# Sparse attention followed by a routed expert layer: key maxima by halving, wide summary scores, new planner figures and smaller filler multiplications

## The chip, the cores and the metric

The kernel runs on one core of one Trainium2 chip. The metric is the device time of one execution in microseconds (us), as the median of several. A core has a matrix engine (TensorE, written PE in the profile; PEld is its weight load), a vector engine (VectorE, DVE), a scalar engine (ScalarE, ACT), a general engine (GpSimd, POOL), a sync engine (SP), and 16 DMA engines. Each engine works through its own queue in order. A later engine waits for an earlier one by semaphores.

## The reference, cut to what matters

There are two stages. The first is attention with 4 batches, 8 heads, 768 positions and 64 dimensions per head. A query sees keys less than 16 positions away, and 24 block summaries, one for each block of 32 positions: the elementwise maximum of the block's keys and the mean of its values.

```
k_sum = k.reshape(B, H, nb, block, D).max(axis=3)
v_sum = v.reshape(B, H, nb, block, D).mean(axis=3)
scores_l = scale * np.matmul(q, k.transpose(0, 1, 3, 2))      # kept where |i - j| < 16
scores_s = scale * np.einsum('bhsd,bhnd->bhsn', q, k_sum) + np.log(block)
...                                                            # softmax over both, times v and v_sum
```

The second stage takes the attention output as 3072 rows of 512. It makes a soft assignment P to 8 experts, with 8 rounds of row and column normalisation, and adds up over the experts.

```
for e in range(E):
    h = np.maximum(x @ w1[e], 0.0)      # 512 -> 1024
    ye = h @ w2[e]                      # 1024 -> 512
    out += P[:, e:e + 1] * ye
```

## The kernel before, in words

**Tiling.** Two heads make a pair, so there are 16 pairs, 4 for each batch. Keys and queries of a pair are transposed to `kT` and `qT`: 128 partitions (two heads of 64 dimensions) by 768 positions. Scores are made with keys on the partitions. The near scores of 128 keys go against 160 queries (`sg`, L344); the summary scores have the 24 block maxima of each head on the partitions (`ss`, L446, L449, L455). Exponentials run on ACT, masks and normalisation on DVE, and the result is transposed into `xT`, which the experts multiply.

**The summary path.** For a pair `key_max` (L332) reduces `kT`, 24 blocks of 32, to `ks` with one DVE reduction. `key_max_split` (L338) spreads `ks` over two heads into `ksT[:, 0:64]`, zero where a row belongs to the other head. For the 12 pairs after the first batch `summaries_2` (L455) makes two multiplications with that 64-column weight: query half 0 goes to partitions 0 to 63 of one PSUM bank, query half 1 to partitions 64 to 127. For the first batch, half 0 uses `ks` directly (L446) and half 1 uses all 128 columns of `ksT` (L449), of which columns 64 to 127 are zero.

**The first batch.** Pairs 0 to 3 are worked in two halves of the queries, so that the first expert's work can begin early. Keys and values of pair 0 come in float32 through SP and are cast on chip. All else comes through POOL's DMA queue, with a cast, in this order: q of pair 0 (half), k and q of pair 1, of pair 2, v of pair 1, k and q of pair 3, v of pairs 2 and 3, two quarters of expert 0's first weight, the other query halves of the four pairs, the other two quarters, k and q of pair 4, expert 0's second weight `w2`. POOL builds the identity and the band mask between the first of these.

**The planner.** Every piece of work is a unit with an engine, a guessed cost in us, dependencies and a priority (`add`). `Plan.order` simulates the engines with these guesses and at each step issues the unit that can start first; among units that can start within 0.02 us the lowest priority number goes first. What it puts out is the program order of every engine. Nothing is decided at run time: a wrong guess only makes an order that fits the real times less well. For the first batch, `plan.follow` fixes the order on PE, DVE and ACT by lists written out by hand; these lists are not in the change. Loads are units on a virtual DMA engine: a load starts after the one before it and takes its guessed transfer time (`load`, L853 and below).

PSUM banks are rings: tag `m` has three banks (transposes of the first batch, its first summary scores, the fillers, and later expert 0's products), `a` three, `s` one pair.

**Fillers.** `keep_busy(n)` issues n multiplications of a zero tile, 128 x 128 weights by 512 columns, into an `m` bank; nothing reads them. Nine are issued at the start, before any input is there. While the planner runs, each time PE would stand idle for over 0.22 us by its figures, it inserts one more (L1268), as long as an `m` bank is free, until expert 0's first evacuation is placed.

**The rest.** Expert 0 takes plain multiplications (L208, L213), which fill PE while the attention pairs 4 to 15 are made. Experts 1 to 7 use a seven-product scheme (L749, L800). The planner orders all of it.

Of the kernel before, what the change touches and what calls it, by code (L numbers as in the profile page):

```python
# [128 lines left out]
def kernel(  # L129
# [10 lines left out]
    nc = tc.nc  # L140
# [82 lines left out]
    with tc.manual_schedule():  # L223
# [15 lines left out]
        ksT = [attn.tile([128, 128], BF16, name=f"ksT{i}") for i in range(NB)]  # L239
# [90 lines left out]
        def key_max(i):  # L330
            r = i % NB
            nc.vector.tensor_reduce(out=ks[r][:, 0, 0:24],  # L332
                                    in_=kT[r][:].rearrange("p (n w) -> p n w", w=32),
                                    axis=AX.X, op=ALU.max)

        def key_max_split(i):
            r = i % NB
            nc.vector.tensor_tensor(out=ksT[r][:, 0:64].rearrange("p (j n) -> p j n", j=2),  # L338
                                    in0=ks[r][:].to_broadcast([128, 2, 32]),
                                    in1=own[:].to_broadcast([128, 2, 32]), op=ALU.mult)  # L340
# [98 lines left out]
        def summaries(i, h, tag):  # L439
            r = i % NB  # L440
            ss, rhs = bank(tag, "ss"), qT[r][:, W + h * HS:W + (h + 1) * HS]
            at["ss", i, h] = ss
            if i < PB and not h:
                for j in range(2):
                    p = slice(64 * j, 64 * j + 64)
                    nc.tensor.matmul(ss[32 * j:32 * j + 32, 0:HS], lhsT=ks[r][p, 0, :], rhs=rhs[p],  # L446
                                     start=True, stop=True)
                return
            nc.tensor.matmul(ss[:, 0:HS], lhsT=ksT[r][:], rhs=rhs, start=True, stop=True)  # L449

        def summaries_2(i):
            r, ss = i % NB, bank("a", "ss")
            for h in range(2):
                at["ss", i, h] = ss[64 * h:64 * h + 64]
                nc.tensor.matmul(ss[64 * h:64 * h + 64, 0:HS], lhsT=ksT[r][:, 0:64],  # L455
                                 rhs=qT[r][:, W + h * HS:W + (h + 1) * HS], start=True, stop=True)
# [147 lines left out]
        def keep_busy(n):  # L604

            t = bank("m", "idle")
            for _ in range(n):
                nc.tensor.matmul(t[:], lhsT=zeros[:, 0:128], rhs=zeros[:], start=True, stop=True)
# [9 lines left out]
        keep_busy(9)  # L618
# [19 lines left out]
        def constants():  # L638
# [10 lines left out]
            for t in ksT:  # L649
                nc.vector.memset(t[:, 64:128], 0.0)  # L650
# [201 lines left out]
        def load_pair(i, parts="kqv"):  # L852
            old = i - NQ  # L853
            for c in parts:
                if c == "v":
                    load(("v", i), lambda: load_v(i), 1.05, 1.85,
                         [U.get(("A", old, 1)), U.get(("near", old))])
                elif i < PB and c in "qr":
                    h = "qr".index(c)
                    load(("q", i, h), lambda h=h: load_qk(i, 1, h), 0.65, 0.65)  # L860
                else:
                    z = "kq".index(c)
                    load((c, i), lambda z=z: load_qk(i, z), 0.75 if i < PB else 1.65,
                         1.2 if i < PB else 1.55, [U.get(("tr", old, z)), U.get(("tr", old, 2))])

        def pair_start(i, prio):
# [9 lines left out]
            for z in range(0 if i >= BY_DMA else 1 if i < PB else 2):  # L876
                buf = Buffer("m" if i < PB else "a")
                U["tr", i, z] = add("PE", 0.5 if i < PB else 0.34, lambda z=z: tr(i, z),
                                    [U["kq"[z], i], U["ident"]] + (war_k, war_q)[z]
                                    + [U["tr", i, 0] if z else ahead], prio, opens=[buf])  # L880
                U["kT", i, z] = add({"ACT": 0.8, "DVE": 0.95 if i < PB else 0.56}, 0,
                                    lambda z=z: tr_out(U["kT", i, z].on, i, z), [U["tr", i, z]], prio,
                                    uses=[buf])
            U["ks", i] = add("DVE", 0.95, lambda: key_max(i), [U["kT", i, 0], U.get(("km", o))], prio)
# [3 lines left out]
            U["vs", i] = add("PE", 0.4, lambda: block_sums(i),  # L888
# [40 lines left out]
        def pair_whole(i, prio):  # L929
# [23 lines left out]
            U["ss", i, 0] = U["ss", i, 1] = add("PE", 0.22, lambda: summaries_2(i),  # L953
# [68 lines left out]
        U["vf32"] = add("LAND", 0, None, [add("RING", 0, None, [])], lag=5.6)  # L1022
# [3 lines left out]
        load_pair(1, "kq")  # L1026
        U["band"] = last[0] = add("POOL", 0.7, band_constants, [last[0]])
        load_pair(2, "kq")
        load_pair(1, "v")
        load_pair(3, "kq")  # L1030
        load_pair(2, "v")
        load_pair(3, "v")
        for n in range(4):
            load(("w1", n), lambda n=n: load_w1(0, n, 4), 0.85, 1.25)
            if n == 1:
                for i in range(PB):
                    load_pair(i, "r")
        load_pair(PB, "kq")
        load("w2", lambda: load_w2(0), 0.85, 5.0)
# [228 lines left out]
        plan.idle = (0.22, lambda: keep_busy(1), U["rl", 0, 0])  # L1268
# [33 lines left out]
```

The softmax here doesn't subtract the row's maximum and nothing guards it: scores larger than these inputs give would overflow.

## Time and profile before

| what | value |
|---|---|
| median of 5 executions | 668.23 us |
| the five | 667.25, 667.77, 668.23, 668.3, 672.26 us |
| the profiled execution | 672.0 us, span from first to last instruction 670.3 us |
| PE busy | 662.2 us, 99% of the span |
| DVE, ACT, POOL busy | 82%, 62%, 30% |
| chain of work that ended last | PE 98% |
| reductions of `key_max` | 16, 948 ns each |
| summary scores of pairs 4 to 15 | 24 multiplications, 350 ns each |
| fillers | 16 |

The page gives busy time by engine, then the span in 40 slices with the granted PE clock in tenths, then the chain that ended last and the costliest groups. In a timeline row the columns are start, length, engine, line, operation, tiles, shape and count, and in brackets the idle time before it and what ended that. In a table of stretches, each engine has its busy time and count, then come the granted PE clock, the DMA share and GB/s. A matmul's length contains its passage through the array, so rows overlap: the cost of one among others is the distance from start to start.

### The profile page before, as it was taken

What the parts mean: (1) busy time and instruction counts of PE and PEld (TensorE: products, weight loads), DVE (VectorE), ACT (ScalarE), POOL (GpSimd) and SP (SyncE); (2) the same over time, 40 slices, a digit from 0 to 9 for tenths busy, and PEclk for the clock granted to TensorE, in tenths of its full rate; (3) what the DMA queues carried; (4) which work ended last, traced back from release to release, by engine and by line L of the source; (5) the groups of instructions that cost most, each with busy time, mean ns of one, the idle gap of its engine ahead of it and who ended that gap; (6) DMA issues with size and microseconds to landing.
All of it is one profiled execution on the core that took longest, in us unless ns stands there. A gap on an engine that the chain in (4) does not pass through costs nothing.

```text
span 670.3 us, 13244 instructions
## 1 busy us (share of the span) xinstructions
PE 662.2 (99%) x5131; PEld 437.7 (65%) x5131; DVE 547.7 (82%) x1030; ACT 415.0 (62%) x773; POOL 198.3 (30%) x256
## 2 busy tenths in 40 slices
PE   8999999999999999999999999999999999999996
PEld 4666665555676666666666666666666666666665
DVE  6789877798989787788779887888778877988776
ACT  5577876565886666656565556656655656556652
POOL 8899522100031221222132222222222113222123
PEclk7899999999999999999999999999999999999999
DMA  9999961610754738375654756473837465334656
GB/s 167 173 141 146 125 92 30 118 21 1 127 94 80 127 61 128 64 116 90 95 95 65 125 86 104 78 126 53 134 68 121 81 100 95 64 63 111 156 135 198
DMA packets 112542, 67.89 MB, mean 101 GB/s; under 512 B 77920, under 2 KB 90464, under 8 KB 112480
## 3 DMA queue, kind: packets, MB, share of 16 engines
q0 software_dynamic: 94800, 57.46, 64.4%
q1 hardware_dynamic: 17152, 9.58, 5.8%
q8 instruction: 40, 0.66, 0.4%
q14 instruction: 22, 0.18, 0.1%
q10 hardware_dynamic: 528, 0.02, 0.0%
HBM read 52.45 MB, written 6.29 MB: 88 GB/s over the span
## 4 chain that ended last, share of the span: by engine, by line
PE 98%; DMA 1%; DVE 0%; issue 0%; ACT 0%; SPq 0%; DVEq 0%
PE yps L800 22%; PE pA L749 22%; PE pY L800 16%; PE pQ L749 11%; PE hps L208 6%; PE yps L213 6%; PE pR L749 5%; PE sg L344 2%; PE vs L352 1%; PE av L504 1%; PE tkq L300 1%; DMA kvf<-in_v_dram 1%; PE tx L542 1%; PE av L430 1%; PE av L436 1%; PE ss L455 1%
## 5 line engine op out<-in xcount | busy, mean ns | idle before, releaser
L800 PEld LDWEIGHTS <-h 128*128 128x128 f16 x2352 | 230.1, 98 | 89.1 <-issue 1.0
L828 POOL DMA_DIRECT2D out_acc<-y x120 | 101.4, 886 | 372.9 <-ACT y L824 96.2
L824 ACT ACTIVATE y<-pY,P_sb 128x256 f32<-128x256 f32 x168 | 80.0, 477 | 124.2 <-PE pY L800 122.4
L815 DVE SCALAR_TENSOR_TENSOR out_acc<-yps,P_sb,out_acc 128x512 f32<-128x512 f32 x128 | 95.4, 746 | 29.3 <-PE yps L800 29.3
L783 DVE TENSOR_TENSOR h<-h 128x1024 f16<-128x1024 f16 x168 | 109.2, 685 | 1.4
L800 PE MATMUL pY<-w,h 128*128 128x256 f16 x672 | 100.0, 273 | 0.6 <-ACT y L824 0.6
L800 PE MATMUL yps<-w2sum,h 128*128 128x256 f16 x672 | 98.4, 273 | 0.0
L749 PE MATMUL pA<-xT,w 128*128 128x512 f16 x336 | 98.3, 379 | 0.0
L800 PE MATMUL yps<-w,h 128*128 128x256 f16 x672 | 93.2, 273 | 0.0
L815 DVE SCALAR_TENSOR_TENSOR out_acc<-pY,P_sb,out_acc 128x512 f32<-128x512 f32 x84 | 62.9, 749 | 31.5 <-PE pY L800 30.0
L749 PEld LDWEIGHTS <-w 128*128 128x128 f16 x672 | 65.8, 98 | 31.5 <-issue 0.2
L749 PEld LDWEIGHTS <-w1sum 128*128 128x128 f16 x504 | 49.3, 98 | 44.3
L771 DVE CUSTOM_DVE_ANT_0 h<-pQ,snap 128x512 f16<-128x512 f32 x84 | 57.7, 687 | 6.1 <-ACT snap L204 3.6
L771 DVE CUSTOM_DVE_ANT_0 h<-pA,snap 128x512 f16<-128x512 f32 x84 | 57.6, 685 | 5.5 <-PE pA L749 5.2
L199 ACT ACTIVATE h<-pA 128x512 f16<-128x512 f32 x84 | 50.7, 603 | 13.1 <-PE pA L749 12.9
L199 ACT ACTIVATE h<-pR 128x512 f16<-128x512 f32 x84 | 50.1, 596 | 8.6 <-PE pR L749 8.1
L204 ACT COPY pR<-pA 128x512 f32<-128x512 f32 x83 | 47.4, 571 | 7.1 <-PE pA L749 6.0
L800 PE MATMUL pY<-w2sum,h 128*128 128x256 f16 x336 | 50.4, 273 | 0.0
L749 PE MATMUL pQ<-xT,w1sum 128*128 128x512 f16 x168 | 50.0, 379 | 0.0
L749 PE MATMUL pA<-xsum,w 128*128 128x512 f16 x168 | 50.0, 379 | 0.0
L749 PE MATMUL pA<-xsum,w1sum 128*128 128x512 f16 x168 | 50.0, 379 | 0.0
L749 PE MATMUL pQ<-xsum,w1sum 128*128 128x512 f16 x168 | 50.0, 379 | 0.0
(147 smaller groups left out, 859.3 us busy)
## 6 DMA issues: line engine op xcount, KB each, us to landing
out_acc<-y POOLq DMA_DIRECT2D x120, 256.0 KB, 3.4
w<-in_moe_w_dram POOLq DMA_DIRECT2D x15, 1024.0 KB, 10.0
out_dram<-out_acc SPq DMA_DIRECT2D x24, 256.0 KB, 2.5
qst<-in_q_dram POOLq DMA_DIRECT2D x32, 96.0 KB, 5.4
vx<-in_v_dram POOLq DMA_DIRECT2D x15, 192.0 KB, 6.1
kst<-in_k_dram POOLq DMA_DIRECT2D x24, 96.0 KB, 5.5
w<-in_moe_w_dram POOLq DMA_DIRECT2D x4, 256.0 KB, 7.2
kst<-in_k_dram POOLq DMA_DIRECT2D x3, 192.0 KB, 4.6
```

The source lines that it names most:

```text
L199: nc.scalar.activation(out=out, in_=in_, func=AF.Relu, bias=0.0, scale=1.0)
L204: (nc.scalar.copy if eng == "ACT" else nc.vector.tensor_copy)(out=out, in_=in_)
L208: nc.tensor.matmul(hp[:, 0:n], lhsT=w1s[e][:, dk, f * 128:(f + 1) * 128], rhs=xT[:, dk, t0:t0 + n], start=(dk == 0), stop=(dk == KD - 1))
L213: nc.tensor.matmul(yp[:, d], lhsT=h[:, f, c * 128:(c + 1) * 128], rhs=w2s[e][:, f, d], start=(f == 0), stop=(f == KF - 1))
L344: nc.tensor.matmul(dst, lhsT=kT[r][p0:p0 + 64, g * 128:(g + 1) * 128], rhs=qT[r][p0:p0 + 64, g * 128 + l0:g * 128 + l1], start=True, stop= ...
L749: nc.tensor.matmul(dst[:], lhsT=lhsT, rhs=rhs, start=first and k == 0, stop=k == HK - 1, skip_group_check=True)
L771: nc.vector._custom_dve(dve_ops.TENSOR_ADD_SAT, out=ring(e, p, q)[:, q % 2, blk, :], in0=at[src, e, p, q][:], in1=at.pop(("snap", n, e, p, ...
L783: nc.vector.tensor_tensor(out=h[:, :, out_, :], in0=h[:, :, a, :], in1=h[:, :, b, :], op=op)
L800: nc.tensor.matmul(dst[:, d], lhsT=lhsT, rhs=rhs, start=f == 0 and n in (1, 5, 2), stop=f == HF - 1, skip_group_check=True)
L815: nc.vector.scalar_tensor_tensor(out=o, in0=y, scalar=scalar, in1=o, op0=ALU.mult, op1=ALU.add)
L824: nc.scalar.activation(out=at[key][:, d], in_=src, func=AF.Copy, bias=0.0, scale=P_sb[:, t, e:e + 1])
L828: nc.gpsimd.dma_start(out=o, in_=at.pop(("y", e, p, c, key))[:], accum_op=ALU.add)
```

## The change

- `key_max`: in place of one reduction over 32, two elementwise maxima on DVE (32 to 16, 16 to 8 columns for each block, into new tiles `k_max`), then a reduction over 8.
- `ksT` is 192 columns wide, with the maxima in columns 64 to 127 and zeros on both sides. `summaries_2` uses a 128-column weight both times, once columns 64 to 191 and once 0 to 127, and adds the two products in the same bank. L449 reads columns 64 to 191. The zeroing at the start covers all 192 columns.
- Fillers have 128 columns in place of 512: 38 at the start in place of 9, and the planner inserts one for each 0.11 us of planned idle time in place of 0.22.
- The planner gets other figures for the loads' transfer times, for `key_max`, for `summaries_2` and for two units of pair 0. The loads of the first batch are issued from one list; item by item it is the order of before.

```
-            nc.vector.tensor_reduce(out=ks[r][:, 0, 0:24],
-                                    in_=kT[r][:].rearrange("p (n w) -> p n w", w=32),
-                                    axis=AX.X, op=ALU.max)
+            src, w = kT[r][:].rearrange("p (n w) -> p n w", w=32), 16
+            for t in k_max:
+                nc.vector.tensor_tensor(out=t[:], in0=src[:, :, 0:w], in1=src[:, :, w:2 * w], op=ALU.max)
+                src, w = t, w // 2
+            nc.vector.tensor_reduce(out=ks[r][:, 0, 0:24], in_=src[:], axis=AX.X, op=ALU.max)
...
             for h in range(2):
                 at["ss", i, h] = ss[64 * h:64 * h + 64]
-                nc.tensor.matmul(ss[64 * h:64 * h + 64, 0:HS], lhsT=ksT[r][:, 0:64],
-                                 rhs=qT[r][:, W + h * HS:W + (h + 1) * HS], start=True, stop=True)
+                nc.tensor.matmul(ss[:, 0:HS], lhsT=ksT[r][:, 64 - 64 * h:192 - 64 * h],
+                                 rhs=qT[r][:, W + h * HS:W + (h + 1) * HS], start=h == 0, stop=h == 1)
...
-                nc.tensor.matmul(t[:], lhsT=zeros[:, 0:128], rhs=zeros[:], start=True, stop=True)
+                nc.tensor.matmul(t[:, 0:128], lhsT=zeros[:, 0:128], rhs=zeros[:, 0:128], start=True, stop=True)
...
-        keep_busy(9)
+        keep_busy(38)
...
-                nc.vector.memset(t[:, 64:128], 0.0)
+                nc.vector.memset(t[:], 0.0)
...
                 if c == "v":
-                    load(("v", i), lambda: load_v(i), 1.05, 1.85,
+                    load(("v", i), lambda: load_v(i), 1.05, {1: 1.85, 4: 2.9}.get(i, 1.5),
...
-                    load(("q", i, h), lambda h=h: load_qk(i, 1, h), 0.65, 0.65)
+                    load(("q", i, h), lambda h=h: load_qk(i, 1, h), 0.65, 2.65 if i + h == 0 else 0.42)
...
-                         1.2 if i < PB else 1.55, [U.get(("tr", old, z)), U.get(("tr", old, 2))])
+                         0.95 if i < PB else 1.75 if i == PB else 1.38, [U.get(("tr", old, z)), U.get(("tr", old, 2))])
...
-                U["tr", i, z] = add("PE", 0.5 if i < PB else 0.34, lambda z=z: tr(i, z),
+                U["tr", i, z] = add("PE", 0.65 if i == 0 else 0.5 if i < PB else 0.34, lambda z=z: tr(i, z),
...
-            U["ks", i] = add("DVE", 0.95, lambda: key_max(i), [U["kT", i, 0], U.get(("km", o))], prio)
+            U["ks", i] = add("DVE", 0.7, lambda: key_max(i), [U["kT", i, 0], U.get(("km", o))], prio)
...
-            U["vs", i] = add("PE", 0.4, lambda: block_sums(i),
+            U["vs", i] = add("PE", 0.65 if i == 0 else 0.4, lambda: block_sums(i),
...
-            U["ss", i, 0] = U["ss", i, 1] = add("PE", 0.22, lambda: summaries_2(i),
+            U["ss", i, 0] = U["ss", i, 1] = add("PE", 0.33, lambda: summaries_2(i),
...
-        U["vf32"] = add("LAND", 0, None, [add("RING", 0, None, [])], lag=5.6)
+        U["vf32"] = add("LAND", 0, None, [add("RING", 0, None, [])], lag=6.4)
...
-            load(("w1", n), lambda n=n: load_w1(0, n, 4), 0.85, 1.25)
...
+        for c in "k1 q1 b0 k2 q2 v1 k3 q3 v2 v3 w0 w1 r0 r1 r2 r3 w2 w3".split():
...
+                load(("w1", i), lambda i=i: load_w1(0, i, 4), 0.85, 1.3)
...
-        load("w2", lambda: load_w2(0), 0.85, 5.0)
+        load("w2", lambda: load_w2(0), 0.85, 4.4)
...
-        plan.idle = (0.22, lambda: keep_busy(1), U["rl", 0, 0])
+        plan.idle = (0.11, lambda: keep_busy(1), U["rl", 0, 0])
```

## The prediction

> **What bounds the kernel now.** I read the page first, then one-microsecond stretches of the start, then the timelines of PE and DVE around what the change touches.
>
> ```profile
> PE 662.2 (99%) x5131; PEld 437.7 (65%) x5131; DVE 547.7 (82%) x1030; ACT 415.0 (62%) x773; POOL 198.3 (30%) x256
> ...
> PEclk7899999999999999999999999999999999999999
> ...
> PE 98%; DMA 1%; DVE 0%; issue 0%; ACT 0%; SPq 0%; DVEq 0%
> ```
>
> PE is never idle after the first 26 us, and from there the order of the work is worth little: only PE's own work counts. What can be won lies in the first slices, where the clock digit is below 9. The stretches (PE, PEld, DVE, ACT, POOL, then PE clock, DMA share, GB/s) and the PE timeline show that:
>
> ```profile
> 6.00:7.00 1.00, 0.31 (x13) 0.27 (x13) 0.16 (x1) 0.63 (x1) 1.00 (x2) 1.00 1.34 211
> 7.00:8.00 1.00, 0.77 (x12) 0.48 (x8) 1.00 (x2) 0.48 (x1) 1.00 (x3) 0.98 1.28 190
> 8.00:9.00 1.00, 1.00 (x12) 0.40 (x8) 0.62 (x2) 0.00 (x0) 1.00 (x2) 0.50 1.27 165
> ...
> 20.00:21.00 1.00, 1.00 (x14) 0.87 (x15) 0.80 (x1) 0.46 (x1) 0.88 (x2) 0.50 1.44 193
> 21.00:22.00 1.00, 1.00 (x9) 0.62 (x6) 0.39 (x2) 0.54 (x1) 1.00 (x2) 0.70 1.52 193
> 22.00:23.00 1.00, 1.00 (x15) 0.59 (x14) 0.80 (x3) 0.33 (x1) 1.00 (x2) 1.00 2.22 160
> ```
>
> ```profile
> 6.69 0.38 PE L309 MATMUL tkq<-ident,qst 64*64 64x64 bf16 x12 [0.90 <-DMA qst<-in_q_dram]
> 7.00 0.39 PE L608 MATMUL idle<-zeros 128*128 128x512 bf16 x1
> 7.62 0.54 PE L352 MATMUL vs<-vx,m_blk 128*128 128x128 bf16 x6 [0.23 <-DVE vx L204]
> 7.96 0.62 PE L608 MATMUL idle<-zeros 128*128 128x512 bf16 x1
> ```
>
> PE waits 0.90 us for the first queries; at 7.96 us the clock falls to half and returns at 21.6 us, 13.65 us later. In that time PE is busy throughout: at half clock it is the bound, and in the chain of waits the fillers at 7.96, 16.4, 19.3 and 21.4 take 0.43 + 0.54 + 0.43 + 0.73 = 2.1 us of it.
>
> **Which execution the sum is made for.** The profiled execution took 672.0 us (span 670.3 and 1.7 around it), 3.8 above the median 668.23. One of the five, 672.26, stands beside it. At full clock the first batch could end far earlier: the last values land at 16.84 (DMA records), and behind them come their block sums 0.54, DVE 0.28, weighted values 0.9, normalisation 0.75, transpose 0.33, copy 0.36, together 3.2, so 20.0 in place of 26.7, where the last copy into `xT` ends. The 3.8 lies within these 6.7. I read the median execution as one in which the clock stayed up for most of this stretch, but no profile of such a one is shown. I make the sum for both.
>
> **Key maxima.** These are DVE rows, two of the timeline and three groups (busy, mean ns, idle before):
>
> ```profile
> 44.00 0.95 DVE L332 TENSOR_REDUCE ks<-kT 128x24 bf16<-128x768 bf16 x1 [0.20 <-ACT kT L204]
> 44.99 0.22 DVE L338 TENSOR_TENSOR ksT<-ks,own 128x64 bf16<-128x64 bf16 x1
> ```
>
> ```profile
> L488 DVE TENSOR_TENSOR Eh<-erh,band 128x960 bf16<-128x960 bf16 x8 | 5.2, 649 | 0.0
> ...
> L419 DVE TENSOR_TENSOR Ee<-er,band 32x80 bf16<-32x80 bf16 x24 | 4.7, 196 | 0.5
> ...
> L571 DVE TENSOR_REDUCE rs_sb<-P_sb 128x24 f32<-128x192 f32 x8 | 2.8, 353 | 1.8 <-ACT P_sb L566 1.6
> ```
>
> Two bf16 elementwise rows, 960 columns in 649 ns and 80 (in runs of 16) in 196, give 0.515 ns a column on a base of 155. The first maximum (384 columns) then takes 353 ns, the second (192) 254. The last reduction has its own row: 192 columns, 353 ns. Each reads what the one before wrote, and the first two rows show what that costs: L338 starts 0.04 us after L332 ends (34 ns in the records), where an independent operation starts 84 ns before the end. So 353 + 34 + 254 + 34 + 353 = 1028 ns against 953: 0.075 longer. The planner's 0.70 is what comes out if all three overlapped like independent ones. Pairs 4 to 15 lie beside a full PE: cost 0, and with that cover gone 12 x 0.075 = 0.9. For pairs 0 to 3 it is hidden while PE is at half clock; at full clock DVE is the denser queue and it costs 4 x 0.075 = 0.3. The other end is the planner's figure, a gain of 4 x 0.25 = 1.0.
>
> [...]
>
> **Wide summary scores.** These are PE rows around one pair of narrow products:
>
> ```profile
> 93.36 0.34 PE L436 MATMUL av<-Ve,Ee 128*128 128x130 bf16 x3
> 93.63 0.35 PE L455 MATMUL ss<-qT,ksT 128*64 128x384 bf16 x2
> 93.92 0.66 PE L208 MATMUL hps<-xT,w 128*128 128x384 f16 x3
> ```
>
> The two narrow products run side by side (starts 3 ns apart). But from the start of the last full-size product before them to their start it is 150 ns, where 130 columns at full clock need 56, and the next starts 286 ns later. Together 436. Two full-width products cost 163 each (eight L208 of 384 columns take 1.30 in the chain), so 56 + 326 = 382: a gain of 54 ns. Where the neighbour before is the 64-row product L344 (4 of 12 pairs), its own 159 stays and it is 159 + 286 against 159 + 326: a loss of 40. 8 x 54 - 4 x 40 = 0.27 us gained, all on the path, since PE is full there. The ends: 12 x 54 = 0.65 gained, 12 x 40 = 0.5 lost, by the order that comes out.
>
> **Fillers.** The start block: nine of 512 columns took 3.72 us (1.26 to 4.98). 38 of 128 columns at 0.107 us each (three L542 take 0.32 at half clock) need 4.06 if the clock stays low, and end at 5.3, about when the first keys are cast (5.21). With the clock up at 4.54, as here, the last seven take 0.055 each (six L300 take 0.33), and they end at 4.95. Cost 0, at most 0.1. The inserted ones: for 0.22 us of planned idle there was one filler of 0.213 at full clock, 0.43 at half; now there are two of 0.055, or two of 0.107. At half clock they lie on the path: 2.1 us become about 1.5, since gaps of 0.11 to 0.22 now get one too. Gain 0.6 in the profiled execution, 0 at full clock, where they stand in true gaps. The wider zeroing adds four times some 0.04 us to DVE at 2.1 us, ahead of a 0.91 wait: 0.
>
> **Planned load times.** The issue order and the DMAs are the same; what moves is where the planner puts PE work that waits for them. By its figures the chain of transfers starts at 4.45 before and 5.5 after. To the last values it is then 11.1 before, 8.96 after, and with 0.9 to land 16.45 before, 15.36 after; the trace has 16.84. The last quarter of the first weight: 24.05 before, 22.24 after; the trace has 23.69. For `w2`: 32.15 before, 29.77 after; the trace has 31.98. The old figures fit this trace, the new ones are 1.5 to 2.2 us early. A product of expert 0 that is placed early stops PE's queue, and behind it the attention work that ACT and DVE wait for. In the profiled execution the first product with `w2` starts at 38.1, 6 us after landing, so nothing is lost there. In one that runs 5 us earlier the stop is between 0 and 2.2 us; I take 0.3, near 0, since the first batch's order is fixed by hand and expert 0's second products have a low priority. If real loads are faster without the profiler this falls away, and a better order could win as much: the lower end is -1.
>
> **The sum.** Profiled execution: -0.27 + 0 - 0.6 + 0 gives 671.1. Median execution: -0.27 + 0.3 + 0 + 0.3 gives 668.23 + 0.3 = 668.5, which I take. I take 0.5% (3.3 us) as what a measurement here can tell from no change.
>
> **The rivals.** *Clock up everywhere (faster).* If the new fillers keep the clock at full through the first batch in every execution, the most is 672.0 - 6.7 (above) - 0.3 = 665.0. For it: 0.90 us without work stands just before the drop, and the planner now knows that these queries come late. Against it: a planned gap now holds half the work, and at most two fillers fit while the first transposes hold their bank.
> *Clock down in most executions (slower).* Activity falls because two small fillers occupy 0.11 of a planned 0.22. If more than half of the executions then lose the clock, the median is the profiled sum, 671.1, and one more stretch as long as a quarter of the 13.65 at half clock adds up to 1.7: 672.8. I set it at 672.
> *The key maxima do get shorter.* Then 668.5 - 1.3 = 667.2; still within 0.5%.
>
> [...]
>
> **How the numbers follow.** No large shift 0.62 (668.5, own range 666.2 to 670.8, of it 0.02 beyond each side of the 0.5%), clock up 0.16 (0.14 under 664.9 with some gain of order), clock down 0.22 (0.16 over 671.6). So faster 0.16, same 0.66, slower 0.18. Leaving out about one in ten on each side the range is 664.4 to 672.6.
>
> **What the profile after will show.** Three DVE rows near 353, 254 and 353 ns with 34 ns between them; L455 as two 128 x 128 products 163 ns apart with no lead-in after a full-size one; the clock digit in the first two slices; whether an L208 or L213 row waits for `w`. The forecast is wrong if the clock stays at half for longer than 13.65 us or never falls in the executions that make the median, or if PE shows a wait of over 1 us after 20 us.

## The result and the profile after

The changed kernel takes 673.69 us (median of 22 executions, 669.23 to 677.39); the kernel before, run beside it, takes 668.3 us (41 executions, 667.18 to 673.7). The ratio of the means is 1.0066, with a 95% interval of 1.0048 to 1.0084: it is slower, by 5.4 us in the median. The forecast of 668.5 us and its range, 664.4 to 672.6, both miss it.

The profiled execution of after took 672.06 us with a span of 670.3 us, so it is one of the better ones. By accident its span equals that of the execution profiled before; that one had lost the clock for 13.65 us and this one for 3.41. The two numbers must not be compared as if nothing had happened. The page of the changed kernel, three lines:

```profile
PE 659.0 (98%) x5159; PEld 439.1 (66%) x5159; DVE 553.6 (83%) x1075; ACT 407.5 (61%) x760; POOL 198.4 (30%) x256
...
PEclk9899999999999999999999999999999999999999
...
PE 88%; DVE 4%; DMA 3%; POOL 2%; issue 1%; SPq 0%; ACT 0%; POOLq 0%; DVEq 0%
```

PE's share of the chain that ended last falls from 98% to 88%: now PE waits, for DVE and for transfers. One-microsecond stretches of after (PE, PEld, DVE, ACT, POOL, then PE clock, DMA share, GB/s) say where:

```profile
6.00:7.00 1.00, 0.38 (x8) 0.11 (x2) 0.12 (x2) 0.80 (x1) 1.00 (x2) 1.00 1.31 201
7.00:8.00 1.00, 0.57 (x16) 0.55 (x17) 0.81 (x2) 0.48 (x2) 1.00 (x3) 1.00 1.31 202
8.00:9.00 1.00, 1.00 (x27) 0.80 (x24) 0.82 (x4) 0.26 (x1) 1.00 (x2) 1.00 1.40 180
...
22.00:23.00 1.00, 0.28 (x3) 0.21 (x3) 1.00 (x5) 0.00 (x0) 1.00 (x2) 0.98 1.97 156
23.00:24.00 1.00, 1.00 (x10) 0.38 (x9) 0.71 (x5) 0.00 (x0) 0.96 (x3) 0.50 2.09 138
```

In the stretch from 6 to 8 us PE is now busy for 0.95 of 2 us, against 1.08 before. The clock, up from 5.90 us in this execution, holds this time and falls at 22.96 us, at the end of the stretch in which PE is busy for 0.28: there it waits 0.87 us for DVE (`xT`). The waits of PE in after (total, times, longest):

```profile
PE hps L208 <- DVE xT L204: 0.9, 1, 0.9
PE tkq L310 <- DMA qst<-in_q_dram: 0.7, 1, 0.7
...
PE hps L208 <- DMA w<-in_moe_w_dram: 0.5, 1, 0.5
PE sg L347 <- DVE kT L204: 0.5, 1, 0.5
PE ss L449 <- DVE ks L337: 0.5, 1, 0.5
PE av L439 <- DMA Ve<-vx: 0.4, 1, 0.4
```

Two of them are products of expert 0 (L208) that stand in PE's queue ahead of what they wait for; one is a summary score that waits for the key maxima (`ks`). Before there was no such row. The rows of the two edits themselves, first the DVE timeline of the first pair, then the PE timeline around two of the twelve pairs of wide scores:

```profile
7.67 0.35 DVE L335 TENSOR_TENSOR kmax<-kT 128x384 bf16<-128x384 bf16 x1
8.05 0.26 DVE L335 TENSOR_TENSOR kmax<-kmax 128x192 bf16<-128x192 bf16 x1
8.34 0.35 DVE L337 TENSOR_REDUCE ks<-kmax 128x24 bf16<-128x192 bf16 x1
```

```profile
52.48 0.38 PE L347 MATMUL sg<-qT,kT 64*128 64x160 bf16 x6
52.80 0.50 PE L458 MATMUL ss<-qT,ksT 128*128 128x384 bf16 x2
53.13 0.49 PE L208 MATMUL hps<-xT,w 128*128 128x384 f16 x2
...
93.52 0.34 PE L439 MATMUL av<-Ve,Ee 128*128 128x130 bf16 x3
93.70 0.49 PE L458 MATMUL ss<-qT,ksT 128*128 128x384 bf16 x2
94.03 0.45 PE L355 MATMUL vs<-vx,m_blk 128*128 128x128 bf16 x5
```

From 7.67 to 8.69 us the three maxima take 1.03 us, as worked out, against 0.95 for the one reduction. The planner was told 0.70. In the records of the two pairs shown, the wide products start 174 and 162 ns apart.

So there are two candidates for the loss. One is the clock: 13 of the 22 executions have a mean granted clock of 0.992 or less (13.65 us at half make 0.990). The other is an order that runs ahead of DVE and of the loads. The experiments had to separate them.

### The profile page after: what moved, and what is told of

It is laid out like the page before. It is cut to its first block, busy times and chain, and to the rows that moved or that the text cites. A ratio compares the mean times of both kernels' runs of the same rounds, so it can differ in the third digit from the quotient of the medians.

```text
span 670.3 us, 13342 instructions
## 1 busy us (share of the span) xinstructions
PE 659.0 (98%) x5159; PEld 439.1 (66%) x5159; DVE 553.6 (83%) x1075; ACT 407.5 (61%) x760; POOL 198.4 (30%) x256
## 4 chain that ended last, share of the span: by engine, by line
PE 88%; DVE 4%; DMA 3%; POOL 2%; issue 1%; SPq 0%; ACT 0%; POOLq 0%; DVEq 0%
PE yps L803 22%; PE pA L752 22%; PE pY L803 16%; PE pQ L752 11%; PE pR L752 5%; PE yps L213 5%; PE hps L208 4%; DMA w<-in_moe_w_dram 1%; DMA vx<-in_v_dram 1%; DMA Ve<-vx 1%; DVE xs L538 1%; PE sg L347 1%; DVE em L410 1%; DVE kmax L335 1%; POOL vx L287 0%
## 5 line engine op out<-in xcount | busy, mean ns | idle before, releaser
L208 PE MATMUL hps<-xT,w 128*128 128x384 f16 x256 | 50.3, 330 | 1.4 <-DVE xT L204 0.9
```

Source lines behind the costliest of these rows:

```text
L208: nc.tensor.matmul(hp[:, 0:n], lhsT=w1s[e][:, dk, f * 128:(f + 1) * 128], rhs=xT[:, dk, t0:t0 + n], start=(dk == 0), stop=(dk == KD - 1))
```

## The experiments

None of these kernels leaves out any of the computation. A kernel's executions are told by the best, the median, and how many lie 2.5 us or more above its own best; for the kernel before, the runs beside the experiments hold 140 executions that differ in time or clock, with the best 667.14, the median 668.6, and 46 so far above. Ten of these drawn at random have a best of 667.1 to 668.1 (95 draws of 100). The best tells mostly of the order of the work, since the clock stays up in it (a mean of 0.998 or more, but not in e9, whose best has 0.988); the count tells mostly of the clock.

| kernel | early filler columns | n | best | median | 2.5 above best | ratio, 95% interval |
|---|---|---|---|---|---|---|
| the change | 384 | 22 | 669.23 | 673.69 | 16 | 1.0048 to 1.0084 |
| e1, small fillers alone | 256 | 10 | 667.01 | 670.2 | 5 | 0.9983 to 1.0044 |
| e2, the change, large fillers | 1024 | 10 | 669.08 | 670.27 | 1 | 0.9990 to 1.0040 |
| e3, load figures alone | 1024 | 10 | 668.23 | 670.76 | 5 | 0.9980 to 1.0037 |
| e4, maxima and wide scores alone | 1024 | 10 | 669.70 | 670.74 | 2 | 1.0004 to 1.0052 |
| e5, maxima alone, figure 0.70 | 1024 | 10 | 669.73 | 670.92 | 3 | 0.9999 to 1.0057 |
| e6, maxima alone, figure 1.03 | 1024 | 10 | 668.23 | 668.81 | 0 | 0.9967 to 1.0019 |
| e7, wide scores alone | 1024 | 10 | 667.80 | 668.86 | 2 | 0.9968 to 1.0029 |
| e8, figure 0.70 alone, no edit | 1024 | 10 | 669.24 | 670.37 | 3 | 0.9992 to 1.0049 |
| e9, the change, figure 1.03 | 384 | 7 | 671.17 | 672.31 | 0 | 1.0028 to 1.0079 |
| e10, e9 with large fillers | 1024 | 10 | 667.89 | 669.45 | 2 | 0.9991 to 1.0030 |
| e11, the change, 256-column fillers | 768 | 10 | 670.04 | 671.05 | 3 | 1.0026 to 1.0058 |
| e12, before, 256-column fillers | 512 | 10 | 667.45 | 670.23 | 6 | 0.9980 to 1.0038 |
| e13, before, 512 columns per 0.11 us | 1024 | 12 | 667.59 | 669.99 | 6 | 0.9995 to 1.0040 |
| e14, e10, old load figures from pair 4 on | 1024 | 12 | 667.04 | 670.18 | 7 | 0.9992 to 1.0043 |
| e15, e10, all old load figures | 512 | 12 | 669.40 | 671.90 | 6 | 1.0009 to 1.0051 |
| e16, before, two fillers put by hand | 1536 | 12 | 667.15 | 668.68 | 3 | 0.9983 to 1.0020 |
| e17, the change, eight fillers put by hand | 1280 | 12 | 669.25 | 670.22 | 3 | 0.9998 to 1.0047 |
| e18, e17 with figure 1.03 | 1280 | 12 | 668.68 | 670.68 | 5 | 1.0015 to 1.0053 |

"Early filler columns" is the number of fillers in the trace that start between the first transpose and 9 us, where PE waits for the first queries and values, times their columns (1024 in the kernel before).

### One part at a time

**e1**: only the fillers change.

```
-                nc.tensor.matmul(t[:], lhsT=zeros[:, 0:128], rhs=zeros[:], start=True, stop=True)
+                nc.tensor.matmul(t[:, 0:128], lhsT=zeros[:, 0:128], rhs=zeros[:, 0:128], start=True, stop=True)
-        keep_busy(9)
+        keep_busy(38)
-        plan.idle = (0.22, lambda: keep_busy(1), U["rl", 0, 0])
+        plan.idle = (0.11, lambda: keep_busy(1), U["rl", 0, 0])
```

> The kernel before with the small fillers alone (38 at the start, one for each 0.11 us of planned idle; all else as before). Theory 'fillers': a small filler keeps PE at work for a quarter of the time of a large one, so the clock falls in more executions and for longer; the median rises to 671.5-674, with mean granted clocks of 0.99 and below in most executions. Theory 'figures' (the planner's new load figures put expert 0's products too early, PE stops and the clock falls because of that): this kernel stays at 667.5-669, and the executions keep the clock of before.

The best, 667.01, is that of before: in themselves the fillers cost nothing. The median is 1.6 above before's, with five of ten executions far above the best; neither theory's range is met, and the interval does not settle it. In the profiled execution (673.31) the records have the clock up for the first time at 27.54 us, though the mean reads 0.998: a count of low means alone misses such executions.

**e2**: the whole change without these three lines, so with the fillers of before.

> The changed kernel with the large fillers of before (9 at the start, 512 columns, one for each 0.22 us); key maxima, wide scores and the planner's figures as changed. Theory 'fillers': back to 668-669.5. Theory 'figures': stays at 672-674, with PE stopped behind a product of expert 0 that waits for its weight at 20 us (0.5 us) and for x at 22 us (0.9 us).

One of ten executions far above the best instead of 16 of 22, and none with a mean clock of 0.992 or less: the median falls by 3.4 us to 670.27. But the best stays at 669.08. So the fillers are the matter for the clock, and something else costs about 2 us even in the best execution.

**e3**: only the planner's figures for loads and the two units of pair 0.

```
-                    load(("v", i), lambda: load_v(i), 1.05, 1.85,
+                    load(("v", i), lambda: load_v(i), 1.05, {1: 1.85, 4: 2.9}.get(i, 1.5),
-                    load(("q", i, h), lambda h=h: load_qk(i, 1, h), 0.65, 0.65)
+                    load(("q", i, h), lambda h=h: load_qk(i, 1, h), 0.65, 2.65 if i + h == 0 else 0.42)
...
-        load("w2", lambda: load_w2(0), 0.85, 5.0)
+        load("w2", lambda: load_w2(0), 0.85, 4.4)
```

> The kernel before with the planner's new figures for loads, for the first transpose and block sums of pair 0 and for the landing of the first values; nothing else. Theory 'figures': 671-674, with first products of expert 0 ahead of the weighted values of pair 3 in PE's queue and PE waits of 0.5 us or more on the first weight's second quarter. Theory 'fillers': within 1.5 us of before, 667-669.7.

The best is 1.1 above before's; PE waits 0.92 us for the neighbours' values (`Ve`) of a later pair. The interval holds no change, and it reaches to 1.0037: from this kernel alone it can't be told whether these figures cost something.

**e4**: the key maxima (with 0.70) and the wide scores together; **e7**: the wide scores alone, which are these edits:

```
-                nc.tensor.matmul(ss[64 * h:64 * h + 64, 0:HS], lhsT=ksT[r][:, 0:64],
-                                 rhs=qT[r][:, W + h * HS:W + (h + 1) * HS], start=True, stop=True)
+                nc.tensor.matmul(ss[:, 0:HS], lhsT=ksT[r][:, 64 - 64 * h:192 - 64 * h],
+                                 rhs=qT[r][:, W + h * HS:W + (h + 1) * HS], start=h == 0, stop=h == 1)
```

> The kernel before with the halved key maxima (planner figure 0.70) and the wide summary scores (0.33); nothing else. Both theories: small, 667.5-669.5; the three DVE operations together 1.03 us from first start to last end, the wide pair 163 ns from start to start. If it is over 671, neither theory holds and the planner's figure of 0.70 (0.33 less than the row) is the cause, by an order that runs ahead of DVE.

> The kernel before with the wide summary scores and their figure 0.33; nothing else. Theory 'wide': 669.5-671 median, best over 668.7. Theory 'order': 668-669.3, best 667-668; by the starts in the traces a wide pair after a 64-row product costs 50 ns more than before and after a full-size one 54 ns less, so within 0.6 us either way over twelve pairs.

e4 shows the 2 us and more (best 669.70, 2.6 above), e7 does not (667.80). So they come with the key maxima.

**e5 and e6**: the key maxima alone, with the planner's figure at 0.70 as in the change, and at the measured 1.03. **e8**: the kernel before with nothing but the figure.

```
-            U["ks", i] = add("DVE", 0.95, lambda: key_max(i), [U["kT", i, 0], U.get(("km", o))], prio)
+            U["ks", i] = add("DVE", 0.7, lambda: key_max(i), [U["kT", i, 0], U.get(("km", o))], prio)
```

> The kernel before with the halved key maxima and the planner's figure 0.70 for them; nothing else. Both of them together with the wide scores gave 670.7 median and 669.7 at best, against 668.7 and 667.2. Theory 'order' (the figure 0.70 is 0.33 below the row, so the planner's order runs ahead of DVE and PE waits): 669.5-671 median, best at or over 668.7. Theory 'wide' (the wide pair costs it): 668-669.3. Theory 'price' (three operations take 0.075 longer): within 0.5 of before.

> The same, but with the planner's figure at 1.03, which is what the three operations take in the profiles. Theory 'order': back to 667.8-669.2, best 667.2-667.8, PE waits on DVE after 30 us under 0.3 us. Theory 'price': as with 0.70. Theory 'wide': 668-669.3.

> The kernel before, with one reduction for the key maxima as it was, but the planner told 0.70 in place of 0.95. No operation is changed, only the order. Theory 'order': 669-670.5 median, best at or over 668.3, since the figure is 0.25 too low here. Theories 'wide' and 'price': as before, 668.3-669, best 667.2.

This is the clearest result on the order. With the same instructions, 0.70 in place of 1.03 costs 1.5 us in the best and 2.1 in the median (e5 less e6). With no instruction changed at all, 0.70 in place of 0.95 costs 2.1 in the best and 1.8 in the median (e8 less before). A wait of PE in e8 that the kernel before does not have:

```profile
PE ss L446 <- DVE ks L332: 0.5, 1, 0.5
```

The planner thinks that DVE is done 0.25 us earlier for each pair, and places no filler ahead of the scores of pair 3, where PE then stands and waits for their maxima. But this row does not show where the 2 us go. PE had no useful work at this place before either: ahead of these scores the kernel before has three fillers from 21.37 us and e13, below, four from 16.88. And in this execution of e8 the clock was at half from 7.70 to 11.11 us. That the figure costs is shown by the times; by which waits, only in part. For the slower instructions no cost can be told: e6 is at 0.9993 of before (0.9967 to 1.0019), though its best lies 1.1 above before's.

### The figure and the fillers within the change

**e9**: the change with 1.03 in place of 0.70. **e10**: the same with the large fillers of before (the lines of e1 undone). **e11**: the change with 256 columns and 19 fillers at the start, one for each 0.11 us as in the change.

> The changed kernel with one figure changed: the planner reckons 1.03 for the key maxima in place of 0.70. Theory 'order plus fillers' (the figure costs 2 us in every execution, the small fillers lose the clock in most executions of the change, each on its own): the best execution falls to 668-668.5, but half of the executions or more still have a mean granted clock of 0.992 or below, so the median is 670.5-673. Theory 'order' alone (the clock is lost because PE runs ahead and waits): hardly any execution loses the clock, median 668.3-669.5.

> The changed kernel with 1.03 for the key maxima and the large fillers of before. Theory 'order plus fillers': 668.2-669.5 median, best 667.5-668.5, no execution with a mean clock of 0.992 or below: as before or 0.5 above, by the new load figures. If it stays at 670 or above, the new load figures cost over 1 us by themselves.

> The changed kernel with fillers of 256 columns (19 at the start, one for each 0.11 us of planned idle as in the change). At full clock one takes 0.107 us, so a planned idle stretch is filled wholly, in as many pieces as in the change. Theory 'amount' (the clock falls since a small filler holds PE for half of its planned time): like the large fillers, 670-671 median, at most 2 of 10 with a mean clock of 0.992 or below. Theory 'pieces' (more fillers, each taking a PSUM bank that real work then has to wait for): like the change, 672-674.

e9 missed its expected best (668 to 668.5): its best is 671.17, and none of its seven executions is near 669. Five have a mean clock of 0.990 or less, from 671.17 to 673.01; the 13 such executions of the change lie from 673.07 up, and the medians of the two groups, 672.31 and 673.92, are 1.6 apart: this much goes with the figure when the clock is lost. e10 has the figure and the fillers put right: best 667.89, median 669.45, ratio 1.0011 (0.9991 to 1.0030), no longer to be told from before; against e2, which has 0.70, its best is 1.2 lower and its median 0.8. e11 lies between. Stretches of e9, in the same columns as above:

```profile
6.00:7.00 1.00, 0.26 (x12) 0.26 (x12) 0.29 (x3) 0.61 (x1) 1.00 (x2) 1.00 1.30 199
7.00:8.00 1.00, 0.51 (x15) 0.48 (x8) 0.97 (x3) 0.48 (x1) 1.00 (x3) 1.00 1.31 198
8.00:9.00 1.00, 1.00 (x19) 0.77 (x18) 0.66 (x3) 0.31 (x1) 1.00 (x2) 0.60 1.33 169
...
21.00:22.00 1.00, 1.00 (x11) 0.47 (x9) 0.81 (x3) 0.14 (x1) 1.00 (x2) 0.58 1.50 182
```

The clock falls at 8.19 us, after two stretches in which PE was busy for 0.26 and 0.51, and returns 13.65 us later.

**e12 and e13** were to say whether size or step of the fillers matters, in the kernel before: e12 has 256 columns, 19 at the start and the step 0.11; e13 has 512 columns and nine, and only the step is 0.11.

> The kernel before with fillers of 256 columns (19 at the start, one for each 0.11 us of planned idle), all else as before. Theory 'amount': no more executions lose the clock than before, gaps of 0.11 to 0.22 us are filled too, so 667.5-668.7 median, best 667.2: equal to before or up to 0.8 better. Theory 'pieces': 670-671 as with 128 columns.

> The kernel before, with its large fillers (9 at the start, 512 columns) but one for each 0.11 us of planned idle in place of 0.22; nothing else. Theory 'amount' (the clock falls when PE holds too little work): more filler work than before, so fewer executions lie 2.5 us or more above the fastest than before (about a quarter of them), under one in seven; the median is 667.6-668.6, the best 667.2-667.8, since a filler of 0.213 us in a gap of 0.11 delays real work a little. Theory 'pieces' (the finer planning makes it worse, whatever the size): median 670-671 as with 128 and 256 columns.

Both were inconclusive. Six of ten and six of twelve executions lie far above the best; for e13 the theory of the amount expected fewer. Its columns in the early wait are those of before and its median is 1.4 above before's, with 1 in the interval. The count of columns is thus not all that decides.

**e14 and e15** put old load figures back into e10: from pair 4 on, with a longer one for `w2`, and all of them.

```
-                    load(("v", i), lambda: load_v(i), 1.05, {1: 1.85, 4: 2.9}.get(i, 1.5),
+                    load(("v", i), lambda: load_v(i), 1.05, {1: 1.85}.get(i, 1.5 if i < PB else 1.85),
-                         0.95 if i < PB else 1.75 if i == PB else 1.38, [U.get(("tr", old, z)), U.get(("tr", old, 2))])
+                         0.95 if i < PB else 1.55, [U.get(("tr", old, z)), U.get(("tr", old, 2))])
-        load("w2", lambda: load_w2(0), 0.85, 4.4)
+        load("w2", lambda: load_w2(0), 0.85, 6.9)
```

> The changed kernel with 1.03 for the key maxima, the large fillers, and the old load figures from pair 4 on (1.55 and 1.85; the figure for w2 at 6.9 so that it is planned to land at 32.2 as before). The new figures of the first batch stay. Theory 'late near values' (the new figures let the planner place the weighted values of pair 4 about 5 us earlier than before, and PE waits 0.9 to 1.6 us for the DMAs that bring the neighbours' values): that wait goes, median 668-668.9, 0.6-1.4 below the version with the new figures (669.45). If the median stays over 669.2, the figures of the first batch cost it.

> The changed kernel with 1.03 for the key maxima, the large fillers and all load figures of before; what stays of the change is the halved key maxima, the wide scores, and 0.65 for the first transpose and block sums of pair 0. Theory 'first-batch figures' (the new figures of the first batch let PE reach pair 4's weighted values before the neighbours' values are there): no PE wait on those DMAs of 0.3 us or more, median 668.2-669.2, best 667.3-668.3, and under a third of the executions 2.5 us or more above the best. If the wait stays, it is the wide scores or the key maxima's figure that move PE there, and the load figures are not the cause.

e10 has one long wait left, 1.6 us for `Ve`, and my theory put it down to the new load figures of the later pairs. e14 speaks against this: the wait is 2.2 us there. e15 fell the other way than expected: with the old figures it became worse, best 669.40 and median 671.90. The new figure for the first queries (2.65) tells the planner that PE will stand idle early; with the old one (0.65) it places a single filler of 512 columns from 5.5 to 9 us. Here is the PE timeline of e15:

```profile
5.22 0.85 PE L298 MATMUL tkq<-ident,kst 128*64 128x128 bf16 x12
6.83 0.53 PE L310 MATMUL tkq<-ident,qst 64*64 64x64 bf16 x12 [0.76 <-DMA qst<-in_q_dram]
```

The two groups of twelve transposes take 0.85 and 0.53 us, where e8, e9 and e17 take 0.38 for the second: the clock is at half. In the records it comes up for the first time at 23.86 us. With the old load figures six of twelve executions have a mean clock of 0.992 or less, and none of ten with the new ones (e10): with large fillers the new figures go with a clock that stays up. That the one missing filler is the reason is not shown, since in this execution the clock was at half already before that place.

### The early wait by itself

e12, e13 and e15 changed more than one thing. The last three kernels put fillers by hand into the one place, between the first transpose of pair 0's keys and that of its queries. **e16** does it in the kernel before with two of 512 columns, **e17** in the change with eight of 128, and **e18** is e17 with the figure at 1.03. The lines of e17:

```
+        gap = Buffer("m")
+        U["i0"] = add("PE", 0.43, lambda: [keep_busy(8)], [U["tr", 0, 0]], -1.0, opens=[gap])
+        first["i"] = lambda i: U["i0"]
...
-                            "T0 Q0 v0 S0 T1 Q1 s0 S1 T2 Q2 s1 A0 S2 v1 T3 A1 Q3 s2 t0 S3 v2 t1 s3 v3 A2 A3 t2 t3".split()])
+                            "T0 i0 Q0 v0 S0 T1 Q1 s0 S1 T2 Q2 s1 A0 S2 v1 T3 A1 Q3 s2 t0 S3 v2 t1 s3 v3 A2 A3 t2 t3".split()])
```

> The kernel before, with two more fillers of 512 columns put by hand on PE between the first transpose of pair 0's keys and that of its queries, where PE waits 0.90 us. If the amount of filler work in this wait decides the clock: the mean granted clock is 0.992 or less in at most 2 of 10 executions (before: about 3 in 10 over 2.5 us above its best), the best stays at 667.1 to 667.7, the median is 667.3 to 668.3. If the amount there is not the cause: the share stays near a third and the median at 668.3 or above. If the fillers get in the way of the first queries' transpose: the best rises by up to 2 x 0.43 = 0.9 us.

> The change, with eight more fillers of 128 columns (1024 columns) put by hand at the same place; size of the fillers, the planner's step of 0.11 and all its figures as in the change. If the amount in the wait decides: a mean clock of 0.992 or less in at most 4 of 10 executions (the change: 13 of 22), median 669.5 to 670.7, best near 669.2, since the 2 us that the figure 0.70 costs stay. If the small pieces or the step decide: the share stays over half and the median at 672 to 674.

> As e17, and with the planner's figure for the key maxima at the measured 1.03. If the two costs (figure 2 us, clock 3 us) make up the whole: best 667.2 to 668, median 667.5 to 669.5, a mean clock of 0.992 or less in at most 4 of 10. If a third cost lies in the other planner figures or in the small pieces: best over 668.5.

**e17** shows the clock's part. None of its twelve executions has a mean clock of 0.992 or less, against 13 of 22 (the two were not run side by side; beside e17 the kernel before had 2 of 29), and the median falls from 673.69 to 670.22; the best stays at 669.25. The PE timeline of e17 from the first transposes on:

```profile
5.67 0.68 PE L611 MATMUL idle<-zeros 128*128 128x128 bf16 x9
6.77 0.38 PE L310 MATMUL tkq<-ident,qst 64*64 64x64 bf16 x12 [0.43 <-DMA qst<-in_q_dram]
7.62 0.50 PE L355 MATMUL vs<-vx,m_blk 128*128 128x128 bf16 x6 [0.47 <-DVE vx L204]
```

The queries' transposes and the block sums start when they do in e9, whose rows are these:

```profile
5.70 0.29 PE L611 MATMUL idle<-zeros 128*128 128x128 bf16 x2
6.74 0.38 PE L310 MATMUL tkq<-ident,qst 64*64 64x64 bf16 x12 [0.75 <-DMA qst<-in_q_dram]
7.61 0.50 PE L355 MATMUL vs<-vx,m_blk 128*128 128x128 bf16 x6 [0.49 <-DVE vx L204]
```

The fillers lie in time in which PE waits anyway; seven more of them, some 0.4 us of work, and in e17's trace the clock stays up, where in e9's it falls at 8.19. The two traces can be compared closely, since the clock comes up at nearly the same moment, 4.78 us in e9 and 4.72 in e17: in the 3.41 us from there PE is busy for 2.14 and 2.50 us. The kernel before and e16 are a second such pair: up at 4.54 and 4.49, busy for 2.00 and 2.15, and only in the first does the clock fall.

The rest of the loss, 670.22 less 668.3, is in the best execution of e17 too (669.25). The waits of its PE:

```profile
PE hps L208 <- DVE xT L204: 0.9, 1, 0.9
PE ss L449 <- DVE ks L337: 0.7, 1, 0.7
...
PE vs L355 <- DVE xs L538: 0.3, 1, 0.3
...
PE ss L458 <- DVE ksT L341: 0.2, 1, 0.2
```

They add up to 2.1 us. The execution of e13 (the kernel before but for the fillers' step), in which the clock stays up, has none of them and a span of 665.9 against 667.7 here. Not all of the 2.1 is lost, though: where PE waits 0.7 for `ks` here, e13 has its four fillers. All in all PE is without useful work, in waits or fillers, for 15.05 us in e17 and 14.05 in e13. That is 1.0 of the 1.8 us; the other 0.8 lies in the multiplications themselves, and its cause is open. With 1.03 (e9, e10, e18) all four are gone.

**e18** missed the expectation that the two parts make up the whole: its best is 668.68 and its median 670.68, no better than e17's. Its waits:

```profile
PE vs L355 <- DMA vx<-in_v_dram: 0.9, 1, 0.9
...
PE av L439 <- DMA Ve<-vx: 0.4, 1, 0.4
```

The 0.9 us is a wait for pair 1's values, which landed at 13.60 us in this execution and at 12.18 in that of e17, though both were issued from 6.12 to 7.18. It is a wait for a transfer in place of a wait for DVE. By the expectation a best over 668.5 speaks for a third cost, in the other figures or in the small pieces; this wait may be it, but no run separates them. Six of the twelve executions have a mean clock of 0.996 or 0.997; no profile shows one of them, and where it falls there stays open.

**e16** met its expectation for the best (667.15) and for the clock (none of 12 at 0.992 or less; with before's 18 of 140 that can still be chance), and missed it for the median, 668.68. Its profile shows where the time goes again: the last copy of the first batch into `xT` ends at 21.9 us in place of 26.7, and PE then waits for the neighbours' values.

```profile
PE av L436 <- DMA Ve<-vx: 1.5, 1, 1.5
```

No version here can be told to be faster than the kernel before.

## Why the prediction was wrong

**The step that failed first is the price of the fillers**: "Cost 0", with a gain of 0.6 in the profiled execution and "0 at full clock". As work on PE that is right (e1's best is 667.01). What the term left out is what the fillers do for the clock. From the first transpose to 9 us 1024 columns of fillers start before (two, at 7.00 and 7.96, behind the 0.90 us wait) and 384 after, and 13 of 22 executions have a mean clock that fits about 13.65 us or more at half. The median execution therefore moved from one with the clock up to one with it down. Large fillers (e2) take off 3.4 of the 5.4 us, and small ones put into the wait (e17) 3.5. This is the rival *clock down in most executions*; it had 0.22. The argument for it stood in the text, "two small fillers occupy 0.11 of a planned 0.22", and I could have counted the columns that the planner's step leaves in that stretch before I gave it so little.

**The second is the planner's 0.70.** I saw that it did not fit the rows, 1.03, and priced only the instructions (0.3). The sentence that failed is "from there the order of the work is worth little", together with the 0.70 taken as a mere error of a guess. An order made from a figure that is 0.25 to 0.33 us too short costs 1.5 to 2.1 us (e5 less e6, e8 less before), with the instructions themselves at no cost that can be told (e6). What is left of the loss in e17, 1.9 of the 5.4, is of this size; which waits make it up is only in part shown. Within the whole change with fillers in the wait the order with 1.03 gains 0.6 in the best and nothing in the median (e18), so the two parts don't simply add up, and a third cost stays open; e10 is the one combination that comes back to before's time.

**The rival's own price** was 671.1 to 672.8, set at 672. With the 2 us of the order added, it would have been 674, near the 673.69 measured; that they add up in such executions is supported by e9 alone, whose five such executions lie 1.6 us below the change's 13.

**The clock-up rival's price.** The first batch was worked out to end at 20.0 us with the clock up. In e13 and e16, where it stays up, the last copy into `xT` ends at 22.3 and 21.9, so of the 6.7 us only 4.4 to 4.8 were there.

**Key maxima.** The duration was right to a few ns: 351, 258 and 353 ns, 1.03 us in all (1028 ns worked out). The rival that they get shorter is out.

**Wide scores.** I took 8 pairs behind a full-size product and 4 behind the 64-row one; the order that came out has 5 and 7. Behind the 64-row product the start-to-start sum is 162 + 172 + 163 = 497 ns against 159 + 3 + 283 = 445 before, a loss of 52 (40 predicted); behind a full-size one of 130 columns 60 + 162 + 162 = 384 against 436, a gain of 52. With these prices for all twelve, in sum 7 x 52 - 5 x 52 = 0.1 us lost where 0.27 gained was predicted, and in e7 nothing that can be told.

**Planned load times.** A product of expert 0 did come to stand too early and waited 0.49 us for the first weight; I took 0.3. The other rows of the kind wait for DVE, and the neighbours' values are late in kernels with old and with new figures (e14, e16). What I had not seen is the other side: the longer figure for the first queries makes the planner place fillers (e15 against e10).

**What the profile after was to show.** The three DVE rows, the pair without a lead-in and an L208 that waits for `w` are there; a wait of over 1 us after 20 us is not, the longest is 0.87. Of the conditions given for being wrong none came as it was worded: the executions that make the median (673.55 and 673.83) have mean clocks of 0.990 and 0.989, about the 13.65 us at half of the profile before. What the forecast had not allowed for is that the median execution is one of these.

## What to carry to other kernels

Filler work must be counted by how much of a waiting stretch it occupies, not by what it costs: the same planned idle time filled to half its amount cost nothing in the best execution and 3.5 us in the median. A planner's cost figure is part of the kernel: measure it in the trace after an edit, because an order made for a shorter operation cost 1.5 to 2.1 us here without any slower instruction. Before two profiles are compared, look at how long the clock was up in each, and run a kernel often enough to see which kind of execution makes its median.

## What the runs showed of the hardware

**In these traces the clock moves in steps of 3.41 us, and falls follow steps with little work.** In the records of these traces the stretches at one clock in the first 50 us last 3.41 us or a multiple: 3.41 (after), 10.24 and 13.65 (before, e9) at half, 3.41 (before, e9) and 17.07 (after) among those at full. Cut all stretches at full clock into steps of 3.41 us, up to 660 us, and add up the columns of the products that start in each, as far as the records hold them. The four steps with 2170 to 3584 columns all end in a fall. Of ten with 4096 to 4608 columns four do, among them before (4096) and e9 (4608). Of the other 3780, with 4774 and more, none does; e17's first has 5312. The falls at 22.96 us in after and at 22.18 in e11 end steps in which PE waits 0.87 us for `xT`, so the order too can cost the clock. This is what 20 traces show together; the border was not tested by a run of its own. A long wait is not needed for it: in e9 the clock fell with none longer than 0.75 us in the step before. The first rise lies anywhere from 4.01 (e12) to 7.28 us (e3) in all traces but those of e1 and e15, whose records have it at 27.54 and 23.86.

**A clock digit of 9 can hide a clock that has not come up yet.** The page of e15 shows 9 in the first slices, a clock of 1.00 in the stretches from 7 to 9 us and a mean clock of 1.0, in an execution of 673.52 us, since the records begin at 23.86 us with the first rise. Before that the distances of the multiplications tell of half speed, as in the row of 0.85 us above. Times near 673.5 with a mean clock of 1.0 occur in the kernel before as well (673.36 to 673.58 in four of the 140 executions).

**Loads land at other times in each trace.** Pair 1's values, issued from about 6.12 to 7.18 us in all 20 traces (each of another kernel), landed between 11.05 (e1) and 13.60 (e18); the first quarter of expert 0's first weight between 17.05 (e5) and 20.32 (e6). No planner's figure can be right for all of these, while the three maxima take 1.02 to 1.04 us for each of the 16 pairs in after.
